# Queries by kv as one float32r pass a head, with the high and low parts stacked in the rows, from the sixth chunk on

## The chip, the core and the metric

The kernel runs on one core of a Trainium2 chip. The core has five engines that work side by side and wait for each other by semaphores: TensorE (PE in the profile; PEld is its loading of weights), VectorE (DVE), ScalarE (ACT), GpSimd (POOL) and SyncE (SP, which issues the DMAs here). TensorE writes to PSUM, eight banks of 2 KB in each of 128 partitions. The metric is the device time of one execution in microseconds (us); less is better.

## What is computed

Linear attention (8 batches, 8 heads, 576 positions, head size 64), then a gated feed-forward block without an activation (model size 512, inner size 1536). Positions of all batches in a row are 4608 tokens.

```python
q_s = softmax(q, over the head's 64 entries)
k_s = softmax(k, over the 576 positions)
kv  = einsum('bhsd,bhse->bhde', k_s, v)          # 64 x 64 a head
x   = einsum('bhsd,bhde->bhse', q_s, kv)         # tokens x 512
out = ((x @ w_a) * (x @ w_b)) @ w_out
```

## The kernel before, in words

**Chunks.** The 4608 tokens are worked through in nine chunks `c` = 0 to 8 of T = 512 tokens; a batch has 576, so all chunks but the first and the last straddle two batches. While TensorE does the feed-forward block of chunk `c`, the attention of chunk `c + 1` is done beside it. "The sixth chunk" is `c = 5`; its attention runs while chunk 4 is multiplied.

**Two float32r parts.** A float32r matmul takes one pass over the columns but keeps fewer bits than float32. So each operand is split (`split`, L338) into a high part (ScalarE copies it into a float32r tile) and a low part (VectorE subtracts the high part from the source), and a product is three passes: high by high, high by low, low by high.

**A chunk's multiplication.** A chunk's loop (L1392) runs over NI = 6 pairs `i` of inner blocks, and in each pair seven products of the Strassen-Winograd kind, 12 matmuls of 256 columns each (`product`, L829), go into three PSUM banks: `kx` (bank k0), `ky` and then `kp` (both bank k1) and `ka` (bank k2). Program order within a pair: attend slice; kx by A11; ky by S2; u2 = ky + kx (L1443 on ScalarE, L1444 on VectorE); ka by S3; u3 (L1447); twelve matmuls of an output projection (`run_pending`, into po0 to po3); attend slice; kp by S1; kx by A12; VectorE's and ScalarE's use of both (L1461 to L1464); another projection; attend slice; kp by S4; L1474 and L1475; ka by A22; L1479 and L1480, and the splits of the gated result. The four remaining banks are po0 to po3; the attention work has one bank, `at`.

**Attention in slices.** `attention_tasks(c)` (L918) returns a list of slices, each a list of steps; `Spread` (L984) hands one slice to each "attend" place of the loop: three a pair, fifteen a chunk, numbered 0 to 14 here (the last pair has none). Slice 3n is at the head of pair n, 3n + 1 in its middle, 3n + 2 in its third place. VectorE's instructions of a slice are queued behind the loop's last VectorE instruction before it (`issue_after`). In slices 0 to 5 keys and values of a new batch are loaded and turned into kv (`key_steps`, `kv_two` L615), and the queries' statistics are taken (`q_stats` L669; `q_stats_out` L682 writes minus the row maxima and the reciprocal sums to DRAM, as `dq`). From the fifth chunk on (`c > 3`) the rest lies so: in slices 8 to 11, for the four head pairs g = 0 to 3, `q_rows` (four DMAs `mr<-dq` that spread maxima and reciprocal sums over the partitions) and `q_turned` (queries with the head's entries in the partitions); in slices 10 to 13 `q_exp` (add the maxima, L722; exponential, L723; split); in slices 11 to 14 `x_product` (L752: three passes with kv's high and low parts as weights; two heads lie side by side in the 128 rows, and kv is a block-diagonal 128x128 matrix made with `mask`) into bank `at`, and L960, where VectorE multiplies by the reciprocal sums into `xf`.

**Order.** For chunks 0 to 2 the order of every engine's queue is written out by hand (`ORDER`, `arrange`). For later chunks the framework's planner sets it at build time, by program order and by its own estimate of when an instruction is ready; on the chip each queue runs in that order. Tiles of one tag share slots (`Slots`), and a new tile waits for the readers of the slot's last one.

Of the kernel before, what the change touches and what calls it, by code (L numbers as in the profile page):

```python
# [255 lines left out]
def linear_attention_then_gated_ffn(  # L256
# [40 lines left out]
    TT = T // P  # L297
    NCH = NT // T
    LATE = NCH - qt_late.shape[0]

    const = ctx.enter_context(tc.tile_pool(name="const", bufs=1))
    sb = ctx.enter_context(tc.tile_pool(name="sb", bufs=2))
# [35 lines left out]
    def split(hi, lo, src, hi_engine="act"):  # L338

        if hi_engine == "act":  # L340
            nc.scalar.copy(out=hi, in_=src)  # L341
        else:
            nc.vector.tensor_copy(out=hi, in_=src)
        return nc.vector.tensor_tensor(out=lo, in0=src, in1=hi.bitcast(F32), op=ALU.subtract)  # L344
# [270 lines left out]
    def kv_two(b, g, kts, vts, tag):  # L615

        pk = ps.tile([P, 2, D + 1], F32, name="pk", tag=tag)
        for n in range(2):
            kv_sums(kts[n], vts[n], tag, pk[:, n])
        den = sb.tile([P, 2], F32, name="den2")  # L620
        nc.vector.tensor_scalar_add(den, pk[:, :, D], EPS)
        nc.vector.reciprocal(out=den, in_=den)
        kv = sb.tile([P, 2, P], F32, name="kv2", bufs=1)
        for n in range(2):
            nc.vector.scalar_tensor_tensor(
                out=kv[:, n].rearrange("p (h d) -> p h d", h=2),
                in0=pk[:, n, 0:D].unsqueeze(1).broadcast_to([P, 2, D]), scalar=den[:, n:n + 1],
                in1=mask.rearrange("p (h d) -> p h d", h=2), op0=ALU.mult, op1=ALU.mult,
            )
        split(*kv_home(b, g), kv, "dve")  # L630


    wholes = sb.tile([P, 2, NP, P], F32, name="wholes", tag="mr", bufs=2)
# [61 lines left out]
    def roomy(c):  # L695
        return c > LATE

# [23 lines left out]
    def q_exp(c, qt, rows):  # L721
        nc.vector.tensor_tensor(out=qt, in0=qt, in1=rows[0], op=ALU.add)  # L722
        nc.scalar.activation(out=qt, in_=qt, func=AF.Exp)  # L723
        if roomy(c):
            hl = sb.tile([P, 2, T], F32R, name="qhl", tag="mr", bufs=2)
            qh, ql = hl[:, 0], hl[:, 1]
        else:
            qh = sb.tile([P, T], F32R, name="qh", bufs=1)
            ql = sb.tile([P, T], F32R, name="ql", bufs=1)
        split(qh, ql, qt)  # L730
        return qh, ql
# [10 lines left out]
    def x_whole(c, g, qw, tag):  # L742

        t0 = c * T
        b0, b1 = t0 // S, (t0 + T - 1) // S
        n0 = min(T, (b0 + 1) * S - t0)
        px = ps.tile([P, T], F32, name="px", tag=tag)
        for b, s in ((b0, slice(0, n0)), (b1, slice(n0, T)))[:b1 - b0 + 1]:
            nc.tensor.matmul(px[:, s], whole[b, g], qw[:, s], start=True, stop=True)  # L749
        return px  # L750

    def x_product(c, g, qhl, tag="at"):  # L752
        qh, ql = qhl
# [164 lines left out]
    def attention_tasks(c):  # L918
# [3 lines left out]
        if c == 2:  # L922
            steps = [(tasks[8][4],)] + steps
            steps[0] += tuple(lambda g=g: kv_split_whole(1, g) for g in range(NP))
            for g in (1, 2, 3):
                load, soft, turn, back, prod = late_key_task(g, "at")
                steps.append((
                    load, lambda soft=soft, turn=turn: (soft(), turn()),
                    lambda back=back, prod=prod: (back(), prod()),
                ))  # L930
        stats, last, turned, rows = [], [], [], []
        every = {}
        for g in range(NP):
# [22 lines left out]
                box["e"] = q_exp(c, box["q"], box["r"])  # L956

            def b2(g=g, box=box):
                px = x_product(c, g, box["e"])
                nc.vector.tensor_tensor(out=xfs[c][:, g], in0=px, in1=box["r"][1], op=ALU.mult)  # L960

# [4 lines left out]
        seq = []  # L966
        for i in range(max(len(stats), len(steps))):
            seq.append((stats[i] if i < len(stats) else []) + (steps[i] if i < len(steps) else []))
        last = pipeline(last)
        if c > 3:  # L970
            begin = 3 * NI - 3 - len(last) - 2
            seq += [[] for _ in range(len(seq), begin)]
            for g in range(NP):
                seq[begin + g:begin + g + 1] = [rows[g:g + 1] + turned[g:g + 1]]
            for n, now in enumerate(last):
                seq[begin + n + 2:begin + n + 3] = [(seq[begin + n + 2] if n + 2 < NP else []) + now]
            return seq
# [414 lines left out]
    for c in range(1, NCH):  # L1392
# [5 lines left out]
        for n, i in enumerate(pairs):  # L1398
            def part(name):
                return named(f"{name}.{(c - 1) * NI + n}") if c < 5 else nullcontext()  # L1400
# [51 lines left out]
            if not end:  # L1452
                with part("proj"):
                    run_pending()
            with part("attend"):
                attend(c > 2 and last)
            kp = ps.tile([P, 2, H], F32, name="kp", tag="k1")
            multiply(kp, S1, T1, True)
            multiply(kx, A12, B21, False)
            with part("pair"):  # L1460
                nc.vector.tensor_tensor(out=cc[:, 3], in0=kp, in1=u3, op=ALU.add)  # L1461
                nc.scalar.copy(out=cc[:, 0, 0], in_=kx[:, 0])  # L1462
# [4 lines left out]
                    run_pending()  # L1467
            if po is None:
                po = [ps.tile([P, DM], F32, name=f"po{t}") for t in range(TT)]
            with part("attend"):  # L1470
                attend(c > 2 and last)
            multiply(kp, S4, B22, False)
# [65 lines left out]
```

## Time and profile before

| | |
|---|---|
| time, median of 3 runs | 936.92 us (936.4 to 938.07) |
| profiled execution, its own time | 935.81 us |
| its span, first to last instruction | 934.0 us |
| TensorE busy | 924.7 us, 6565 matmuls |
| VectorE busy | 618.0 us, 1218 instructions |
| ScalarE busy | 394.0 us, 1094 instructions |
| GpSimd busy | 107.9 us, 88 instructions |
| HBM read and written | 213.09 MB and 36.93 MB |

The page of the profile gives busy time by engine, the chain of work that ended last, and the costliest groups of instructions with the idle time before them and what ended it. Other views of the same trace are used below: the groups by line and shape, the waits, the timeline of one engine (rows: start, time, engine, line, operation, out<-in, shape, count, and in brackets the idle time before and what ended it), and the busy time of each engine in chosen windows.

### The profile page before, as it was taken

What the parts mean: (1) busy time and instruction counts of PE and PEld (TensorE: products, weight loads), DVE (VectorE), ACT (ScalarE), POOL (GpSimd) and SP (SyncE); (2) the same over time, 40 slices, a digit from 0 to 9 for tenths busy, and PEclk for the clock granted to TensorE, in tenths of its full rate; (3) what the DMA queues carried; (4) which work ended last, traced back from release to release, by engine and by line L of the source; (5) the groups of instructions that cost most, each with busy time, mean ns of one, the idle gap of its engine ahead of it and who ended that gap; (6) DMA issues with size and microseconds to landing.
All of it is one profiled execution on the core that took longest, in us unless ns stands there. A gap on an engine that the chain in (4) does not pass through costs nothing.

```text
span 934.0 us, 17535 instructions
## 1 busy us (share of the span) xinstructions
PE 924.7 (99%) x6565; PEld 835.2 (89%) x6565; DVE 618.0 (66%) x1218; ACT 394.0 (42%) x1094; POOL 107.9 (12%) x88
## 2 busy tenths in 40 slices
PE   8999999999999999999999999999999999999998
PEld 6677789999988999999999999999999999999997
DVE  7998898788854677467656574666657454753433
ACT  8988774435521345133613271324424352322111
POOL 1654434330000000000100010000000000000000
PEclk9999999999999999999999999999999999999999
DMA  9989889989788879983989289945997389627761
GB/s 349 349 308 367 333 321 337 330 310 285 266 305 291 259 270 345 283 330 110 337 255 380 94 302 297 361 169 198 331 320 247 102 293 308 219 96 270 248 224 47
DMA packets 88947, 253.27 MB, mean 271 GB/s; under 512 B 10720, under 2 KB 11296, under 8 KB 88864
## 3 DMA queue, kind: packets, MB, share of 16 engines
q1 hardware_dynamic: 88864, 252.16, 78.5%
q8 instruction: 52, 0.85, 0.4%
q14 instruction: 31, 0.25, 0.1%
HBM read 213.09 MB, written 36.93 MB: 268 GB/s over the span
## 4 chain that ended last, share of the span: by engine, by line
PE 95%; DVE 2%; DMA 1%; ACT 0%; POOL 0%; issue 0%; SPq 0%; DVEq 0%; POOLq 0%
PE po L864 31%; PE kx L835 14%; PE kp L835 14%; PE ka L835 14%; PE pt L805 7%; PE ky L835 7%; PE px L761 2%; PE pk L582 2%; PE po L850 1%; PE px L749 1%; DMA kt_first<-in_kt 1%; DVE xo L344 0%; POOL mx L512 0%; DVE kt L544 0%; DVE mc L1128 0%
## 5 line engine op out<-in xcount | busy, mean ns | idle before, releaser
L864 PE MATMUL po<-wo_w,gh 128*128 128x512 f32 x840 | 264.5, 396 | 0.0
L835 PE MATMUL kx<-xo,ws 128*128 128x256 f32 x1152 | 184.7, 282 | 0.3 <-DVE cc L1463 0.2
L835 PE MATMUL ka<-xo,ws 128*128 128x256 f32 x1152 | 177.7, 282 | 0.7 <-DVE u L1447 0.4
L835 PE MATMUL kp<-xo,ws 128*128 128x256 f32 x1152 | 174.8, 283 | 0.5 <-DVE cc L1461 0.5
L864 PEld LDWEIGHTS po<-wo_w,gh 128*128 128x128 f32 x840 | 151.3, 188 | 25.1 <-ACT gh L341 0.5
L835 PEld LDWEIGHTS kx<-xo,ws 128*128 128x128 f32 x1152 | 160.7, 189 | 6.7 <-DVE cc L1463 0.7
L835 PEld LDWEIGHTS ka<-xo,ws 128*128 128x128 f32 x1152 | 157.9, 189 | 6.7 <-issue 0.6
L835 PEld LDWEIGHTS kp<-xo,ws 128*128 128x128 f32 x1152 | 155.7, 189 | 5.8 <-DVE cc L1461 0.8
L864 PE MATMUL po<-wo_w,gl 128*128 128x512 f32 x420 | 153.0, 396 | 0.0
L341 ACT CAST gh<-cc 128x512 fp32r<-128x512 f32 x96 | 58.6, 620 | 168.8 <-DVE cc L1475 145.4
L1462 ACT COPY cc<-kx 128x256 f32<-128x256 f32 x48 | 17.8, 372 | 177.6 <-PE kx L835 170.4
L864 PEld LDWEIGHTS po<-wo_w,gl 128*128 128x128 f32 x420 | 78.0, 188 | 15.7 <-DVE gl L344 0.4
L1474 DVE TENSOR_TENSOR cc<-kp,u 128x512 f32<-128x512 f32 x48 | 33.1, 690 | 86.0 <-PE kp L835 85.9
L805 PE MATMUL pt<-xo,ws 128*128 128x512 f32 x288 | 87.0, 418 | 0.0
L835 PE MATMUL ky<-xo,ws 128*128 128x256 f32 x576 | 86.6, 281 | 0.0
L675 ACT ACTIVATE qt<-qt,st 128x64 f32<-128x64 f32 x224 | 75.3, 340 | 19.6 <-DVE st L672 18.7
L835 PEld LDWEIGHTS ky<-xo,ws 128*128 128x128 f32 x576 | 76.8, 189 | 1.1
L344 DVE TENSOR_TENSOR gl<-cc,gh 128x512 fp32r<-128x512 f32 x96 | 67.1, 704 | 12.9 <-ACT gh L341 12.8
L1461 DVE TENSOR_TENSOR cc<-kp,u 128x512 f32<-128x512 f32 x48 | 33.2, 691 | 62.7 <-PE kp L835 62.2
L805 PEld LDWEIGHTS pt<-xo,ws 128*128 128x128 f32 x288 | 52.9, 188 | 17.3 <-issue 4.2
L512 POOL PARTITION_ALL_REDUCE mx<-m x20 | 18.1, 910 | 433.0 <-DVE m L523 433.0
L1443 ACT COPY u<-kx 128x512 f32<-128x512 f32 x48 | 28.0, 583 | 51.5 <-PE kx L835 48.0
(150 smaller groups left out, 1117.3 us busy)
## 6 DMA issues: line engine op xcount, KB each, us to landing
ws<-dw SPq DMA_DIRECT2D x260, 512.0 KB, 6.0
dw<-ws SPq DMA_DIRECT2D x42, 512.0 KB, 6.6
mr<-dq SPq DMA_DIRECT2D x112, 128.0 KB, 6.0
raw<-in_w_ab SPq DMA_DIRECT2D x24, 512.0 KB, 7.8
out<-ot SPq DMA_DIRECT2D x36, 256.0 KB, 4.7
vt<-in_v SPq DMA_DIRECT2D x28, 325.0 KB, 6.1
qt<-in_q SPq DMA_DIRECT2D x32, 256.0 KB, 5.1
kt<-in_k SPq DMA_DIRECT2D x24, 320.0 KB, 5.3
```

The source lines that it names most:

```text
L341: nc.scalar.copy(out=hi, in_=src)
L344: return nc.vector.tensor_tensor(out=lo, in0=src, in1=hi.bitcast(F32), op=ALU.subtract)
L512: nc.gpsimd.partition_all_reduce(out_ap=mx, in_ap=kv_max(kt), channels=P, reduce_op=bass_isa.ReduceOp.max,)
L582: nc.tensor.matmul(pk[h * D:(h + 1) * D], kt[:, j, h], vt[:, j, h], start=(j == 0), stop=(j == J - 1),)
L675: nc.scalar.activation(out=qt[:, j, h], in_=qt[:, j, h], func=AF.Exp, bias=st[:, h, 0, j:j + 1], accum_out=st[:, h, 1, j:j + 1],)
L761: nc.tensor.matmul(px[:, s], w, m[:, s], start=(i == 0), stop=(i == 2))
L805: nc.tensor.matmul(pt, w[:, wp], x[g][:, xp], start=(g == 0 and i == 0), stop=(g == NP - 1 and i == 2),)
L835: ins = nc.tensor.matmul(pt[:, n], w[:, n, wp, c], x[:, xp, c], start=(first and n == 0 and i == 0), stop=(i == 5), skip_group_check=True,)
L864: ins = nc.tensor.matmul(po[t], a[:, ts], wo[f][:, w], start=(f == ends[0] and i == 0), stop=(f == ends[1] and i == 2),)
L1443: nc.scalar.copy(out=u2, in_=kx)
L1461: nc.vector.tensor_tensor(out=cc[:, 3], in0=kp, in1=u3, op=ALU.add)
L1474: nc.vector.tensor_tensor(out=cc[:, 1], in0=kp, in1=u2, op=ALU.add)
```

## The change

- From `c = 5` on, `q_exp` writes one tile a head h: the high part of the head's 64 rows into these rows, the low part into the other 64 rows (four half-height instructions instead of two of full height).
- `kv_tall` makes matching weights for each head: in the head's own rows the high part of kv beside its low part, in the other rows the high part again beside zeros. `kv_two` leaves out the mask; `kv_again` rebuilds the weights of the batch that the sixth chunk shares with the fifth.
- `x_tall` replaces `x_product`: for each head one pass a batch, instead of three passes for both heads together. The result's own 64 rows and the other 64 rows have to be added: ScalarE copies the other rows out of PSUM (into the tile of the maxima, used up by then) and VectorE adds. Then L960's multiplication takes both heads at once from SBUF.
- The second bank that this needs is bank k1 in a pair's middle slice and k0 in its third slice. To this end kx by A12 stands ahead of kp by S1 in chunks 4 to 8.
- For `c >= 5` products are in slices 8, 10, 11, 13 (before: 11 to 14), `q_exp` one slice earlier each (7, 9, 10, 12; before 10 to 13), rows and turned queries in slices 6, 7, 8, 10 (before 8 to 11).

```diff
+    TALL = 5
@@ in kv_two, after the reciprocal
+        if b * S >= TALL * T:
+            kv = sb.tile([P, 2, P], F32, name="kv2", bufs=1)[:, :, 0:D]
+            nc.vector.tensor_tensor(
+                out=kv, in0=pk[:, :, 0:D], in1=den.unsqueeze(2).broadcast_to([P, 2, D]), op=ALU.mult,
+            )
+            kv_tall(b, g, [(kv[own(h)], None) for h in range(2)])
+            return
@@ new functions
+    def own(h):
+        return slice(h * D, (h + 1) * D)
+    def kv_tall(b, g, heads):
+        q = g // 2
+        w = [sb.tile([P, 2, P], F32R, name=f"kvt{x}{q}", tag=f"kv{x}{q}") for x in "hl"]
+        for n in (2 * q, 2 * q + 1):
+            kvs[b, n] = tuple(t[:, n % 2] for t in w)
+        for h, (hi, lo) in enumerate(heads):
+            me, it = own(h), own(1 - h)
+            nc.vector.tensor_copy(out=w[h][me, :, me], in_=hi)
+            nc.scalar.copy(out=w[h][it, :, me], in_=hi)
+            if lo is None:
+                nc.vector.tensor_tensor(
+                    out=w[h][me, :, it], in0=hi, in1=w[h][me, :, me].bitcast(F32), op=ALU.subtract
+                )
+            else:
+                nc.vector.tensor_copy(out=w[h][me, :, it], in_=lo)
+            nc.gpsimd.memset(w[h][it, :, it].bitcast(F32), 0.0)
+    def kv_again(b):
+        for g in range(0, NP, 2):
+            kvh, kvl = kv_parts[b, g // 2]
+            kv_tall(b, g, [[x.bitcast(F32)[own(h), :, own(h)] for x in (kvh, kvl)] for h in range(2)])
@@ in q_exp, after the exponential
+        if c >= TALL:
+            hl = sb.tile([P, 2, T], F32R, name="qhl", tag="mr", bufs=2)
+            for h in range(2):
+                split(hl[own(h), h], hl[own(1 - h), h], qt[own(h)])
+            return hl
@@ new, in x_product's place for c >= TALL
+    def x_tall(c, g, hl, rows, xf):
+        t0 = c * T
+        edge = min((t0 // S + 1) * S - t0, T)
+        for h, tag in enumerate((at["spare"], "at")):
+            px = ps.tile([P, T], F32, name=f"px{h}", tag=tag)
+            for s in (slice(0, edge), slice(edge, T))[:1 + (edge < T)]:
+                nc.tensor.matmul(
+                    px[:, s], kvs[(t0 + s.start) // S, g][h], hl[:, h, s], start=True, stop=True
+                )
+            me = own(h)
+            nc.scalar.copy(out=rows[0][me], in_=px[own(1 - h)])
+            nc.vector.tensor_tensor(out=xf[me], in0=px[me], in1=rows[0][me], op=ALU.add)
+        nc.vector.tensor_tensor(out=xf, in0=xf, in1=rows[1], op=ALU.mult)
@@ in attention_tasks
+        if c == TALL and c * T % S:
+            steps = [(lambda: kv_again(c * T // S),)] + steps
+            if c >= TALL:
+                seq += [[] for _ in range(len(seq), 3 * NI - 3)]
+                for g, n in enumerate((8, 10, 11, 13)):
+                    exp, mul = every["last"][g]
+                    n_load = max(n - 3, 6)
+                    seq[n_load] = seq[n_load] + [rows[g], turned[g]]
+                    seq[n - 1] = seq[n - 1] + [exp]
+                    seq[n] = [mul] + seq[n]
+                return seq
@@ in the loop over pairs
+            at["spare"] = "k1"
             with part("attend"):
                 attend(c > 2 and last)
+            if c + 1 >= TALL:
+                multiply(kx, A12, B21, False)
             kp = ps.tile([P, 2, H], F32, name="kp", tag="k1")
             multiply(kp, S1, T1, True)
-            multiply(kx, A12, B21, False)
+            if c + 1 < TALL:
+                multiply(kx, A12, B21, False)
...
+            at["spare"] = "k0"
             with part("attend"):
                 attend(c > 2 and last)
             multiply(kp, S4, B22, False)
```

More of the change, by code (lines that the diff above doesn't have):

```diff
@@ L958, in b2 @@
             def b2(g=g, box=box):
+                if c >= TALL:
+                    x_tall(c, g, box["e"], box["r"], xfs[c][:, g])
+                    return
                 px = x_product(c, g, box["e"])
@@ L968, in attention_tasks @@
             seq.append((stats[i] if i < len(stats) else []) + (steps[i] if i < len(steps) else []))
+        every["last"] = last
         last = pipeline(last)
         if c > 3:
+            if c >= TALL:
+                seq += [[] for _ in range(len(seq), 3 * NI - 3)]
[6 more added lines that the diff above has]
+                return seq
             begin = 3 * NI - 3 - len(last) - 2
```

## The prediction

> **What bounds the kernel now.** First the page: its span, the busy shares, and the chain of work that ended last.
>
> ```profile
> span 934.0 us, 17535 instructions
> PE 924.7 (99%) x6565; PEld 835.2 (89%) x6565; DVE 618.0 (66%) x1218; ACT 394.0 (42%) x1094; POOL 107.9 (12%) x88
> PE 95%; DVE 2%; DMA 1%; ACT 0%; POOL 0%; issue 0%; SPq 0%; DVEq 0%; POOLq 0%
> ```
>
> TensorE is busy 99% of the span and makes 95% of the last chain. Then the busy time by engine in the four stretches in which the attention of chunks 5 to 8 is done beside the multiplication of chunks 4 to 7 (window, its length, then busy us of PE, PEld, DVE, ACT, POOL, with counts).
>
> ```profile
> 436.00:535.00 99.00, 99.00 (x753) 91.87 (x752) 62.71 (x130) 36.31 (x111) 3.72 (x4) 1.00 0.78 267
> 535.00:635.00 100.00, 100.00 (x755) 93.22 (x754) 63.53 (x130) 36.66 (x111) 3.73 (x4) 1.00 0.77 264
> 635.00:735.00 100.00, 100.00 (x757) 92.93 (x757) 63.70 (x131) 36.70 (x111) 3.72 (x4) 1.00 0.76 256
> 735.00:831.00 96.00, 96.00 (x663) 89.07 (x663) 54.53 (x104) 34.00 (x107) 0.00 (x0) 1.00 0.70 231
> ```
>
> TensorE never rests there; VectorE has some 36 us free of 99, ScalarE 63. The granted clock is 1.00. Last, TensorE's waits over the whole span; outside of the start this is the longest (one time, 0.5 us).
>
> ```profile
> PE kp L835 <- DVE cc L1461: 0.5, 1, 0.5
> ```
>
> So a matmul taken out of this part shortens the run by its pitch (start to start), as long as nothing new makes TensorE wait. That decides this change: it takes matmuls away and adds work to the two engines that have room, in places where TensorE depends on them.
>
> The Trainium skill (Perfetto Trace Analysis, section Identifying the Most-Contended Engine) warns that a busy share of matmuls is no measure of the headroom of TensorE, since they are pipelined. By that rule the 99% alone proves nothing; the near absence of waits, above, and the even pitches, below, speak for TensorE all the same.
>
> **What is removed.** The timeline of TensorE around one query product in each stretch: its first row, and the first row of what follows.
>
> ```profile
> 497.99 0.45 PE L761 MATMUL px<-qhl,kvh 128*128 128x320 f32 x2
> ...
> 498.73 1.57 PE L835 MATMUL kp<-xo,ws 128*128 128x256 f32 x12
> ...
> 597.46 0.52 PE L761 MATMUL px<-qhl,kvh 128*128 128x384 f32 x2
> ...
> 598.27 0.69 PE L835 MATMUL kp<-xo,ws 128*128 128x256 f32 x4
> ...
> 697.04 0.56 PE L761 MATMUL px<-qhl,kvh 128*128 128x448 f32 x2
> ...
> 697.89 0.84 PE L835 MATMUL kp<-xo,ws 128*128 128x256 f32 x5
> ...
> 794.15 0.62 PE L761 MATMUL px<-qhl,kvh 128*128 128x512 f32 x2
> ...
> 794.84 0.28 PE L835 MATMUL ka<-xo,ws 128*128 128x256 f32 x1
> ```
>
> One head pair's product holds TensorE for 0.74, 0.81, 0.85 and 0.69 us: three passes over 512 columns, in one or two pieces. Afterwards it is two passes over the same pieces, with weights of the same 128x128 form, so a third goes: 0.25, 0.27, 0.28 and 0.23 us. Four head pairs a chunk: 4 x 1.03 = **4.1 us** off TensorE. Nothing else on TensorE changes in number.
>
> The Trainium skill (TensorE: Matmul & The Clock Gate, section Wait — 56ns, not 53.3ns?) gives a warm matmul's start to start as its columns at 2.4 GHz plus about 2.5 ns. By that, sixteen passes of 512 columns are an estimated 3.5 us; the rows give 0.23 us a pass (794.15 to 794.84 for three), a little more, and the measurement is taken.
>
> **What is added, beside TensorE.** Groups by line and shape (busy, mean ns): VectorE's low part (both sources in SBUF) and ScalarE's high part, the multiplication by the reciprocal sums (one source in PSUM), a ScalarE copy out of PSUM, and two VectorE copies out of PSUM of 64 and of 128 rows.
>
> ```profile
> L344 DVE TENSOR_TENSOR qhl<-qtt,qhl 128x512 fp32r<-128x512 f32 x24 | 16.6, 690 | 15.8 <-ACT qhl L341 15.7
> L341 ACT CAST qhl<-qtt 128x512 fp32r<-128x512 f32 x24 | 14.9, 620 | 0.6
> L960 DVE TENSOR_TENSOR xf<-px,mr 128x512 f32<-128x512 f32 x28 | 19.3, 689 | 24.5 <-PE px L761 19.2 <-DMA ws<-dw 3.8 <-DMA kt<-in_k 0.9
> L1443 ACT COPY u<-kx 128x512 f32<-128x512 f32 x48 | 28.0, 583 | 51.5 <-PE kx L835 48.0 <-DVE cc L1474 1.8 <-DVE kvl L344 1.7
> L688 DVE COPY sst<-pst 64x128 f32<-64x128 f32 x7 | 2.0, 281 | 12.1 <-PE pst L686 12.1
> L569 DVE COPY kt<-pkb 128x128 f32<-128x128 f32 x4 | 1.1, 285 | 0.4 <-PE pkb L567 0.4
> ```
>
> The trace has no half-height instruction of 512 elements. The last two rows bound it: 64 rows take 281 ns where 128 take 285, so I charge half height at the full price; at the other end, half of it. Per head pair VectorE gets one more subtraction and two additions (3 x 0.69 = 2.1 us), ScalarE one more cast and two copies (0.62 + 2 x 0.58 = 1.8 us). That is 8.3 and 7.1 us a chunk, well inside the free time above. The weights of `kv_tall` replace a split of the same size by instructions of 64 rows (some 0.3 us each, by the 281 ns row), in slices where TensorE is not waiting for them: nothing. `kv_again` happens once, some eight short VectorE instructions, 2 to 3 us, chunk 4's first slice: between 0 and 1 us on the path, taken as 0.
>
> Averages don't decide, places do. Busy time in pairs 2, 3 and 4 of chunk 5:
>
> ```profile
> 569.40:585.20 15.80, 15.80 (x134) 14.69 (x131) 6.84 (x16) 1.98 (x4) 0.00 (x0) 1.00 0.97 280
> 585.20:602.30 17.10, 17.10 (x121) 16.05 (x120) 10.54 (x19) 5.12 (x9) 0.00 (x0) 1.00 1.04 353
> 602.30:619.60 17.30, 17.30 (x122) 16.22 (x122) 12.28 (x22) 6.08 (x11) 0.00 (x0) 1.00 0.76 286
> ```
>
> Counting VectorE's instructions of `q_exp` and of the product by slice: pair 2 goes from 0 to 6, pair 3 from 5 to 12, pair 4 from 7 to 6. At 0.69 us: 6.84 + 4.1 = 11.0 of 15.8 us, 10.54 + 4.8 = 15.3 of 17.1, 12.28 - 0.7 = 11.6 of 17.3. **Pair 3 becomes tight for VectorE (90%)**, with a slack pair on each side.
>
> **New waits.** (a) In slices 10 and 13 the first product lies in bank k1, and kp by S1 waits until ScalarE has copied and VectorE has added: 0.58 + 0.69 = 1.3 us after the product. Behind these instructions nothing else of TensorE's stands but the second product (about 0.25 us) and the moved kx by A12; twelve such matmuls take 1.44 us by these rows:
>
> ```profile
> 477.07 1.60 PE L835 MATMUL kp<-xo,ws 128*128 128x256 f32 x12
> 478.51 1.20 PE L835 MATMUL kx<-xo,ws 128*128 128x256 f32 x9
> ```
>
> Cover 1.7 against 1.3: a margin of 0.4 us, if both engines are free when the product ends. If one instruction is in the way it is gone by 0.2 to 0.3. Eight such places. (b) In slices 8 and 11 the first product lies in k0; the readers of kx are done long before, and the next kx comes after kp by S4 and ka by A22, 2 x 1.44 = 2.9 us: covered. (c) With kx ahead of kp, L1461 comes up to 1.1 us later; kp by S4 waits for it, behind a projection of twelve matmuls (2.8 us, twelve at 0.23): covered. Of kx's twelve matmuls only nine (the row of 478.51) come behind kp there: the planner already puts three of them first.
>
> (d) **Row maxima.** The DMAs of the first head pair, and VectorE in pair 2 of chunk 4:
>
> ```profile
> 467.50 0.47 SPq L690 DMA_DIRECT2D dq<-sst  x1
> ...
> 470.19 8.24 SPq L716 DMA_DIRECT2D mr<-dq  x8
> DMA to landing us min/median/max: 3.8/7.3/8.8
> 474.15 0.69 DVE L1447 TENSOR_TENSOR u<-ka,u 128x512 f32<-128x512 f32 x1
> 478.71 0.69 DVE L1461 TENSOR_TENSOR cc<-kp,u 128x512 f32<-128x512 f32 x1 [3.87 <-PE kp L835]
> ```
>
> SyncE already issues them at 470.2, right after `dq`; naming slice 6 can't make that much earlier, so no SP queue is newly blocked. They land around 472.0 + 7.3 = 479.3 (fourth issue some 1.8 us after the first). Slice 7, behind L1447, could use them at 474.8. If the planner queues the addition there, VectorE stands until 479.3 instead of 478.7: L1461 is late by 0.6 + 0.7 = 1.3 us, its projection still covers it, and slice 8's product comes after about 482.6 (0.7 + 0.63 + 2 x 0.62 + 0.7 later). Bounds 0 and 1 us a chunk; taken as 0.25.
>
> **Sum.** Minus 4.1; plus (a) half a margin lost at a time, 8 x 0.1 = 0.8; plus (d) some 0.2 to 0.3. About **-3.1 us**. The profiled execution took 935.81 us, 1.8 above its span, so it would come to 932.7; the median of the runs shown is 1.1 higher than that execution, so I predict 936.92 - 3.1 = **933.8 us**.
>
> **Rivals.**
>
> 1. *The gain is eaten by readers of the px banks.* VectorE, at 90% in pair 3 and strictly in order, or ScalarE, comes to the readers one instruction late (0.69 us): each of eight places costs 0.3, and pair 3's general lag about as much in three of four chunks: 936.9 - 4.1 + 2.4 + 1 = 936.2. For it: pair 3's load; against: the planner has hidden such hand-overs almost without a wait so far.
> 2. *Slower: the hand-over of bank k1 in slices 10 and 13.* If both engines are each an instruction behind (0.69 + 0.62 = 1.3), kp by S1 waits 0.9 us, eight times: 7.3 us, and the run takes 936.9 - 4.1 + 7.3 = 940.1. It decides from 0.5 us of wait a place (4.1 / 8), that is from readers 0.9 us late.
> 3. *No gain at all.* If the pitch of the matmuls that follow is held by something that removed passes don't shorten (weight loads are busy 89%), it stays at 936.9. The even pitches speak against it. The Trainium skill's warning above, of busy shares, would allow it.
> 4. *Full gain:* nothing waits and the spread-out slices remove the last small waits: 936.9 - 4.1 - 0.5 = 932.3.
>
> **How the numbers follow.** Forecast, around 933 to 935: 50%. Rival 1: 22%. Rival 2 and smaller forms of it above 938.8: 15%. Rival 3: 5%. Rival 4: 8%. A run of this kernel can tell 0.2% (1.9 us) from no change. Faster by more than that (below 935.05): the forecast, rival 4 and 0.01 of rival 1, 0.59; slower: rival 2 and 0.02 of rival 1, 0.17; within it the rest, 0.24. Range 932.0 to 939.2: it takes in the full gain, rival 1 and rival 3, and leaves out some 0.03 below and most of rival 2, 0.13, above.
>
> **What would show it.** Right: 56 matmuls of px where chunks 5 to 8 had 84, about 8.2 us of them by pitch instead of 12.4; 48 more VectorE instructions there; no wait of kp for ScalarE or VectorE over 0.5 us; L722 not waiting for `mr<-dq` by more than 2 us. Wrong: waits of TensorE in pairs 3 and 4 that add up to more than 2 us, kp by S1 waiting for the px addition, kx by A11 of pair 3 waiting for slice 8's, or half-height instructions that take more than the full-height ones.

## The result: slower, by about 1%

The changed kernel took 945.8 us (median of six runs, 943.25 to 949.52) against 936.85 us for the kernel before beside it (six runs, 935.62 to 938.07): a ratio of 1.0097, with a 95% interval of 1.0075 to 1.012. Forecast was 933.8, with a range up to 939.2. The profiled execution took 943.25 us, the fastest of the six; 7.4 us above the profiled execution of before.

**The page of the profile after** (span; busy time; the last chain by engine):

```profile
span 941.3 us, 17611 instructions
PE 927.1 (98%) x6537; PEld 834.2 (89%) x6537; DVE 652.4 (69%) x1280; ACT 430.8 (46%) x1158; POOL 111.3 (12%) x104
PE 89%; DVE 6%; DMA 3%; issue 1%; ACT 1%; POOL 0%; SPq 0%; DVEq 0%; POOLq 0%
```

TensorE ran 28 matmuls fewer and is still at 98%. That line alone hides the loss. The chain shows it: TensorE's share fell from 95% to 89%, VectorE's rose from 2% to 6%.

**The removed matmuls are gone.** The windows of before, for the px matmuls alone (busy us and count of PE, PEld, DVE, ACT):

```profile
436.00:535.00 99.00, 3.15 (x16) 2.47 (x16) 5.50 (x8) 4.66 (x8) 1.00 0.77 267
...
735.00:831.00 96.00, 3.22 (x8) 1.51 (x8) 5.50 (x8) 4.66 (x8) 1.00 0.69 231
```

Four windows hold 16 + 16 + 16 + 8 = 56, where before had 84.

**Where the time went.** TensorE's waits in chunks 4 to 7 of the changed kernel, 437 to 840 us; the same view of before has no row at all:

```profile
PE px L799 <- DVE qhl L345: 1.6, 3, 0.5
PE kp L890 <- DVE cc L1535: 1.5, 3, 0.7
PE ky L890 <- DVE cc L1549: 1.1, 5, 0.5
PE kx L890 <- ACT qhl L342: 0.6, 1, 0.6
PE px L799 <- DVE u L1514: 0.4, 1, 0.4
```

(Line numbers after: L890 is the product, L799 a tall pass, L803 ScalarE's copy, L804 VectorE's addition, L805 the multiplication, L1535 the sum that takes in kp by S1, before L1461, and L1549 the one that takes in kp by S4, before L1474.) A wait lengthens the distance from start to start by more than its own time: the 0.42 us ahead of kp at 606.36 us (below) made it 0.58 us longer than usual. So I also counted stalls by starts: of each two neighbouring matmuls, the time from start to start less the median for that form, where more than 0.06 us is left, added up over pairs 3 and 4 of chunks 4 to 7. That gives 9.8 us after and 0.5 before. Of the 9.8 us, 2.3 lie ahead of matmuls of kp, 2.8 ahead of ky, 3.0 ahead of px and 1.5 ahead of kx. And it closes: 4.1 us fewer matmuls, 9.3 us more stalls, 5.2 us longer by reckoning; measured by ScalarE's copies of kx, from pair 5 of chunk 3 to pair 0 of chunk 8, it took 5.6 us longer. The other 1.7 us of the profiled difference arose ahead of the fourth chunk, where both kernels do the same (last section).

**The place is pair 3.** Busy time in pairs 2, 3 and 4 of chunk 5 after, same columns as in the prediction:

```profile
569.40:589.00 19.60, 19.60 (x171) 18.34 (x170) 12.23 (x26) 5.74 (x11) 0.00 (x0) 1.00 0.80 253
589.00:609.30 20.30, 19.88 (x141) 18.57 (x141) 16.95 (x29) 11.83 (x20) 0.40 (x2) 1.00 1.00 395
609.30:626.00 16.70, 16.00 (x109) 14.54 (x108) 13.70 (x24) 5.12 (x9) 0.40 (x2) 1.00 0.60 206
```

Pair 3 was to hold 15.3 us of VectorE's work in 17.1; it holds 16.95 in 20.3. Now TensorE through it (the output projection's rows left out), first before, then after:

```profile
592.17 1.59 PE L835 MATMUL kp<-xo,ws 128*128 128x256 f32 x12
593.61 1.24 PE L835 MATMUL kx<-xo,ws 128*128 128x256 f32 x9
...
598.27 1.64 PE L835 MATMUL kp<-xo,ws 128*128 128x256 f32 x12
599.75 1.59 PE L835 MATMUL ka<-xo,ws 128*128 128x256 f32 x12
601.17 0.40 PE L835 MATMUL kx<-xo,ws 128*128 128x256 f32 x2
...
602.21 1.40 PE L835 MATMUL kx<-xo,ws 128*128 128x256 f32 x10
603.45 1.59 PE L835 MATMUL ky<-xo,ws 128*128 128x256 f32 x12
```

```profile
599.65 0.41 PE L799 MATMUL px<-qhl,kvth 128*128 128x384 f32 x2
...
600.92 1.11 PE L890 MATMUL ka<-xo,ws 128*128 128x256 f32 x8
601.88 0.39 PE L799 MATMUL px<-qhl,kvth 128*128 128x384 f32 x2
602.11 0.69 PE L890 MATMUL ka<-xo,ws 128*128 128x256 f32 x4
602.64 1.59 PE L890 MATMUL kp<-xo,ws 128*128 128x256 f32 x12
604.07 0.40 PE L799 MATMUL px<-qhl,kvtl 128*128 128x384 f32 x2
604.30 1.64 PE L890 MATMUL ka<-xo,ws 128*128 128x256 f32 x12
606.36 1.69 PE L890 MATMUL kp<-xo,ws 128*128 128x256 f32 x12 [0.42 <-DVE cc L1535]
607.94 1.66 PE L890 MATMUL kx<-xo,ws 128*128 128x256 f32 x12
610.14 0.47 PE L799 MATMUL px<-qhl,kvtl 128*128 128x384 f32 x2 [0.55 <-DVE qhl L345]
610.77 1.70 PE L890 MATMUL ky<-xo,ws 128*128 128x256 f32 x12 [0.16 <-DVE cc L1549]
```

Bank k1 holds, in turn, kp by S1, kp by S4 and the next ky, and VectorE has to read each before the next may be written. Before, kp by S1 stands 7 us into the pair (592.17, from 585.2) and a whole projection lies between it and kp by S4; behind that, ka by A22, a product and the next kx give 3.7 us until ky. After, k1 is lent to px at 599.65, and the planner queued kp by S1 behind both projections and ka by A22, 13.6 us into the pair (602.64, from 589.0). Nothing waits there. But what used to lie between the three users of k1 is spent: it takes the next pair's ka by S3 (604.30) as filler, and kp by S1, its sum, kp by S4, its sum and ky become a nearly bare chain: one product of twelve matmuls is left in each gap (ka, then kx). VectorE in that stretch:

```profile
600.71 1.41 DVE L804 TENSOR_TENSOR xf<-px,mr 64x512 f32<-64x512 f32 x2 [2.12 <-ACT mr L803]
602.15 0.69 DVE L805 TENSOR_TENSOR xf<-xf,mr 128x512 f32<-128x512 f32 x1
...
603.49 0.68 DVE L833 TENSOR_TENSOR xt<-xf 128x512 f32<-128x512 f32 x1
...
605.62 0.69 DVE L1535 TENSOR_TENSOR cc<-kp,u 128x512 f32<-128x512 f32 x1
606.22 0.69 DVE L345 TENSOR_TENSOR xo<-xt,xo 128x512 fp32r<-128x512 f32 x1
...
607.15 1.41 DVE L804 TENSOR_TENSOR xf<-px,mr 64x512 f32<-64x512 f32 x2
608.59 1.40 DVE L345 TENSOR_TENSOR qhl<-qtt,qhl 64x512 fp32r<-64x512 f32 x2
610.03 0.69 DVE L1549 TENSOR_TENSOR cc<-kp,u 128x512 f32<-128x512 f32 x1
```

VectorE stood 2.12 us for ScalarE's copy at 598.6 to 600.7 (which itself had waited for px up to 600.1), and then never rests up to 610.7. kp by S1 ended at 604.2, its sum starts at 605.6; kp by S4 ended at 608.05, its sum starts at 610.03, behind two additions and two subtractions of the new work. Those delays are what TensorE waits for. The experiments ask which of the three makes the loss: the load, the standing for ScalarE, or the chain on k1.

### The profile page after: what moved, and what is told of

Same layout as the page of the kernel before. It is cut to its first block, busy times and chain, and to the rows that moved or that the text cites. A ratio compares the mean times of both kernels' runs of the same rounds, so it can differ in the third digit from the quotient of the medians.

```text
span 941.3 us, 17611 instructions
## 1 busy us (share of the span) xinstructions
PE 927.1 (98%) x6537; PEld 834.2 (89%) x6537; DVE 652.4 (69%) x1280; ACT 430.8 (46%) x1158; POOL 111.3 (12%) x104
## 4 chain that ended last, share of the span: by engine, by line
PE 89%; DVE 6%; DMA 3%; issue 1%; ACT 1%; POOL 0%; SPq 0%; DVEq 0%; POOLq 0%
PE po L919 30%; PE kx L890 13%; PE kp L890 13%; PE ka L890 13%; PE pt L860 7%; PE ky L890 7%; PE pk L583 2%; DMA ws<-dw 1%; PE po L905 1%; PE px L816 1%; PE px L789 1%; DMA qtt<-in_q_late 1%; DVE xo L345 1%; DVE qhl L345 1%; DVE xf L804 1%
## 5 line engine op out<-in xcount | busy, mean ns | idle before, releaser
L890 PE MATMUL kx<-xo,ws 128*128 128x256 f32 x1152 | 181.0, 282 | 1.0 <-ACT qhl L342 0.6
L890 PE MATMUL ka<-xo,ws 128*128 128x256 f32 x1152 | 179.5, 283 | 0.7 <-DVE u L1517 0.4
L890 PE MATMUL kp<-xo,ws 128*128 128x256 f32 x1152 | 172.1, 282 | 2.0 <-DVE cc L1535 2.0
L890 PEld LDWEIGHTS kx<-xo,ws 128*128 128x128 f32 x1152 | 159.1, 189 | 7.4 <-ACT qhl L342 0.8
L890 PEld LDWEIGHTS ka<-xo,ws 128*128 128x128 f32 x1152 | 158.6, 189 | 7.0 <-issue 0.6
L890 PEld LDWEIGHTS kp<-xo,ws 128*128 128x128 f32 x1152 | 154.1, 189 | 7.0 <-DVE cc L1535 2.9
L919 PE MATMUL po<-wo_w,gl 128*128 128x512 f32 x420 | 150.8, 396 | 0.0
L919 PEld LDWEIGHTS po<-wo_w,gl 128*128 128x128 f32 x420 | 77.9, 188 | 15.3 <-DVE gl L345 0.4
L890 PE MATMUL ky<-xo,ws 128*128 128x256 f32 x576 | 87.8, 283 | 1.1 <-DVE cc L1549 1.1
L890 PEld LDWEIGHTS ky<-xo,ws 128*128 128x128 f32 x576 | 76.8, 189 | 3.6 <-DVE cc L1549 2.3
L1549 DVE TENSOR_TENSOR cc<-kp,u 128x512 f32<-128x512 f32 x48 | 33.1, 689 | 65.1 <-PE kp L890 64.8
L1535 DVE TENSOR_TENSOR cc<-kp,u 128x512 f32<-128x512 f32 x48 | 33.1, 690 | 32.3 <-PE kp L890 31.9
```

What stands on the lines that cost most here:

```text
L890: ins = nc.tensor.matmul(pt[:, n], w[:, n, wp, c], x[:, xp, c], start=(first and n == 0 and i == 0), stop=(i == 5), skip_group_check=True,)
L919: ins = nc.tensor.matmul(po[t], a[:, ts], wo[f][:, w], start=(f == ends[0] and i == 0), stop=(f == ends[1] and i == 2),)
L1549: nc.vector.tensor_tensor(out=cc[:, 1], in0=kp, in1=u2, op=ALU.add)
```

## The experiments

Each ran beside the kernel before on the same chip. Ratios are to it, with 95% intervals; edits are against the changed kernel unless said otherwise. "Stalls" are those in pairs 3 and 4 of chunks 4 to 7 counted as above (before: 0.5 us).

### The pieces that are free: slices, swap, load

New slices with the old product (TALLX = 99 turns off tall weights, tall product and swap):

```diff
-        if c >= TALL:
+        if c >= TALLX:
             hl = sb.tile([P, 2, T], F32R, name="qhl", tag="mr", bufs=2)
```

> The slices alone: products of chunks 5 to 8 in slices 8, 10, 11, 13, exponentials one slice earlier, row maxima from slice 6, with the old three-pass product in one bank, the old drain and the old order of kx and kp. Theory A (VectorE and ScalarE have too much to do in pair 3, because of the added half-height instructions): the places cost little, 935 to 939 us. Theory B (the new places and the earlier row maxima are themselves what costs): most of the 9 us, 942 to 946 us.

Measured 937.38 us, 1.0003 (0.9993 to 1.0012): nothing.

The swap alone, in the kernel before:

```diff
+            if c + 1 >= 5:
+                multiply(kx, A12, B21, False)
             kp = ps.tile([P, 2, H], F32, name="kp", tag="k1")
             multiply(kp, S1, T1, True)
-            multiply(kx, A12, B21, False)
+            if c + 1 < 5:
+                multiply(kx, A12, B21, False)
```

> Only kx by A12 ahead of kp by S1 in chunks 4 to 8, all else as before the change. Theory A: nothing, 936 to 938 us. Theory C (the swap delays kp's sum on VectorE and with it the next products): 940 us or more.

Measured 937.2 us, 1.0004 (0.9995 to 1.0013): nothing.

The load on VectorE alone: new slices, old product, and spare half-height additions behind it, eight a chunk; then one more in each exponential, twelve a chunk, as many as the change adds.

```diff
+                if c >= TALL:
+                    for h in range(2):
+                        r = [box["r"][w][own(h)] for w in range(2)]
+                        nc.vector.tensor_tensor(out=r[0], in0=r[0], in1=r[1], op=ALU.add)
```

> The new slices with the old three-pass product (which alone took 937.4 us), and behind each product two more half-height VectorE additions, on rows that are used up: 8 VectorE instructions a chunk, with no ScalarE work, no bank and nobody waiting for them. If VectorE's number of instructions in these places is the cause: 941 to 944 us. If it is the chain over ScalarE and the banks: 937 to 938.5 us.

> The new slices with the old product, two spare half-height VectorE additions behind each product (as the earlier run with 8 a chunk, 936.7 us) and one more in each exponential step: 12 spare VectorE instructions a chunk, as many as the change adds, with no ScalarE work and no chain. If VectorE's number of instructions alone fills pair 3 (it was at 14.5 busy us of 17.2 there with 24 instructions, 28 would be 17): 939 to 942 us. If the queue's waits for ScalarE are needed as well: 936.5 to 938 us.

Measured 936.73 us, 1.0015 (1.0005 to 1.0024), and 937.17 us, 1.0004 (0.9995 to 1.0013): little or nothing with eight, nothing with twelve. Pair 3 of chunk 5 with twelve spares:

```profile
587.20:604.70 17.50, 17.50 (x123) 16.45 (x123) 15.37 (x27) 5.60 (x10) 0.00 (x0) 1.00 1.02 401
```

VectorE is at 88% there, near the 90% forecast for the change, and TensorE doesn't lose a moment. The number of instructions alone is not the cause.

### The drain in parts

Without any drain (the multiplication reads the second pass alone), with only the borrowed bank read, without ScalarE's copies, and with ScalarE's copies but without VectorE's additions:

```diff
-            me = own(h)
-            nc.scalar.copy(out=rows[0][me], in_=px[own(1 - h)])
-            nc.vector.tensor_tensor(out=xf[me], in0=px[me], in1=rows[0][me], op=ALU.add)
-        nc.vector.tensor_tensor(out=xf, in0=xf, in1=rows[1], op=ALU.mult)
+        nc.vector.tensor_tensor(out=xf, in0=px, in1=rows[1], op=ALU.mult)
```

> The change, but the result of the second head's pass alone is multiplied by the reciprocal sums: the two ScalarE copies and the two half-height additions a head pair are left out, and the first pass has no reader. Theory A: with 8 VectorE and 8 ScalarE instructions a chunk fewer, and no chain behind the banks, most waits of TensorE go: 932 to 937 us. Theories B and C: 942 to 946 us.

```diff
+            if h == 0:
+                nc.vector.tensor_tensor(out=xf, in0=px, in1=rows[1], op=ALU.mult)
```

> As the kernel without the drain, but the one multiplication reads the first head's pass, in the borrowed bank k0 or k1, and the second pass has no reader. If the hold of the borrowed bank costs by itself (the wait at kp by S1 in slices 10 and 13 that the prediction's second rival had): 3 to 7 us more than there, 940 to 944 us. If not: 936 to 938 us.

```diff
-            nc.scalar.copy(out=rows[0][me], in_=px[own(1 - h)])
```

> The change without ScalarE's copies of the other rows: the additions read the unchanged row maxima instead (so half of each sum is left out), VectorE's instruction count is that of the change, and it waits for TensorE alone. If it is the chain TensorE, ScalarE, VectorE at the head of VectorE's queue that costs: 937 to 940 us. If it is the number of VectorE instructions: 943 to 946 us.

```diff
             nc.scalar.copy(out=rows[0][me], in_=px[own(1 - h)])
-            nc.vector.tensor_tensor(out=xf[me], in0=px[me], in1=rows[0][me], op=ALU.add)
-        nc.vector.tensor_tensor(out=xf, in0=xf, in1=rows[1], op=ALU.mult)
+        nc.vector.tensor_tensor(out=xf, in0=px, in1=rows[1], op=ALU.mult)
```

> The change without VectorE's two additions a head pair: ScalarE copies as in the change, and VectorE multiplies the second pass alone (so the first head's result and the sums are left out). If VectorE's instructions cost: 936 to 939 us, near the kernel without any drain. If ScalarE's copies and the hold of the banks by them cost: 942 us or more.

| what is left of the drain | us | ratio (95%) | stalls |
|---|---|---|---|
| one multiplication, second pass | 936.61 | 1.0003 (0.9993 to 1.0012) | 2.7 |
| one multiplication, borrowed bank | 936.92 | 0.9992 (0.998 to 1.0004) | 3.5 |
| VectorE's part | 941.12 | 1.0039 (1.0024 to 1.0054) | 7.8 |
| ScalarE's part, one multiplication | 941.69 | 1.0046 (1.0029 to 1.0063) | 7.4 |
| all of it (the change) | 945.8 | 1.0097 (1.0075 to 1.012) | 9.8 |

So the whole loss hangs on the drain, and each engine's part brings about half of it. Borrowing the bank is not dear in itself if one instruction frees it. With that shortest hold TensorE still has kp by S1 behind the projections, but VectorE comes to its sum sooner, and a product is left to cover the next step, as the timeline of pair 3 of chunk 5 shows:

```profile
600.41 1.59 PE L888 MATMUL kp<-xo,ws 128*128 128x256 f32 x12
...
602.78 1.69 PE L888 MATMUL kp<-xo,ws 128*128 128x256 f32 x12 [0.55 <-DVE cc L1533]
604.31 1.58 PE L888 MATMUL ka<-xo,ws 128*128 128x256 f32 x12
605.73 1.59 PE L888 MATMUL kx<-xo,ws 128*128 128x256 f32 x12
607.16 1.59 PE L888 MATMUL ky<-xo,ws 128*128 128x256 f32 x12
```

Here the next pair's ka by S3 still stands between kp by S4 and ky, where the change had used it one place earlier.

### Moving work off VectorE, or elsewhere in time

Each of these gives VectorE less to do, or fewer instructions ahead of its sums. All were slower than the kernel before.

```diff
-        nc.vector.tensor_tensor(out=xf, in0=xf, in1=rows[1], op=ALU.mult)
+        nc.gpsimd.tensor_tensor(out=xf, in0=xf, in1=rows[1], op=ALU.mult)
```

> The change, with the last multiplication by the reciprocal sums on GpSimd instead of VectorE: 4 VectorE instructions a chunk fewer, and the drain of the banks as it was. Theory A in the form 'VectorE's total load': a third of the added load goes, 941 to 944 us. If it is the drain of the banks or the queue ahead of it that counts: 945 us, unchanged.

Measured 948.57 us, 1.0115 (1.009 to 1.014); stalls 15.5 us, some 3 of them from matmuls at half clock (last section).

```diff
-        nc.vector.tensor_tensor(out=qt, in0=qt, in1=rows[0], op=ALU.add)
+        (nc.gpsimd if c >= TALL else nc.vector).tensor_tensor(out=qt, in0=qt, in1=rows[0], op=ALU.add)
```

> The change with the addition of the row maxima on GpSimd: four full-height VectorE instructions a chunk fewer, ahead of the exponential, where no bank is held. If VectorE's load in pair 3 is the cause, about a third goes as with the other instructions left out: 941 to 944 us. If a longer chain to the split counts more (GpSimd took 1.3 us for such an instruction, VectorE 0.7): 946 us or more.

Measured 946.04 us, 1.0098 (1.0062 to 1.0134). Stalls in pairs 3 and 4 fell to 4.4 us, but kx now waited 5.3 us for the additions of slice 8's px (bank k0). GpSimd takes 1.29 us for what took VectorE 0.69:

```profile
481.34 1.29 POOL L757 TENSOR_TENSOR qtt<-qtt,mr 128x512 f32<-128x512 f32 x1 [0.37 <-DMA mr<-dq]
```

Both on GpSimd (the reciprocal sums taken in ahead of the split, since the product is linear), exponentials two slices ahead, products in 10, 11, 13, 14:

```diff
+            nc.gpsimd.tensor_tensor(out=qt, in0=qt, in1=rows[1], op=ALU.mult)
...
-                for g, n in enumerate((8, 10, 11, 13)):
+                for g, n in enumerate((10, 11, 13, 14)):
```

> The change with both full-height steps on GpSimd: the row maxima added there, and the multiplication by the reciprocal sums done there too, before the split instead of after the sum; exponentials two slices ahead of the products, which are in slices 10, 11, 13, 14. VectorE has 16 instructions a chunk instead of 24 (12 before the change). If VectorE's load in pair 3 is the cause: 933 to 938 us, level with the kernel before or under it. If not: 943 us or more.

Measured 954.23 us, 1.0197 (1.0175 to 1.0219). TensorE's waits in chunks 4 to 7 now include 4.5 us of kx for ScalarE's copy into u and 4.6 us of ky for the sum of kp by S4.

ScalarE empties both halves of each bank (four copies a head pair), and VectorE adds and multiplies at full height, from SBUF, one slice later:

```diff
-            nc.vector.tensor_tensor(out=xf[me], in0=px[me], in1=rows[0][me], op=ALU.add)
+            nc.scalar.copy(out=xf[me], in_=px[me])
+    def x_join(rows, xf):
+        nc.vector.tensor_tensor(out=xf, in0=xf, in1=rows[0], op=ALU.add)
```

> The change with VectorE taken out of the drain: ScalarE copies both halves of each pass out of PSUM (four half-height copies a head pair instead of two), and VectorE adds and multiplies at full height from SBUF one slice later, when the copies are long done (two instructions a head pair instead of three). VectorE then never stands at the head of its queue for a product. If those waits, together with the work behind them, are the loss: 934 to 938 us. If ScalarE's part of the chain, or the split ahead of the products, is: 941 us or more.

Measured 956.58 us, 1.0202 (1.0156 to 1.0248), the worst; stalls 19.7 us (some 3 of them again at half clock), mostly of px waiting for `qhl` and of ky waiting for the sum of kp by S4.

The preparation of the next chunk's operands (L833 and the splits of `xo`, which the earlier products draw into pair 3) kept behind the loop's VectorE work; products of the last two head pairs later; and both:

```diff
-                    x_operands(xfs[c + 1], early, xo)
+                    with tc.issue_after(last.ins) if c + 1 >= 5 else nullcontext():
+                        x_operands(xfs[c + 1], early, xo)
```

> The change, with VectorE's preparation of the next chunk's operands (x_operands) queued behind VectorE's work of pair 4 (early ones) and behind u3 of pair 5 (late ones) for chunks 5 to 8, so that none of it can stand in pairs 3 and 4. Theory D (the products that now come earlier draw this preparation forward into pair 3, where the added drains and splits already fill VectorE's queue, and sums that TensorE needs come late): about half of the loss goes or more, 938 to 942 us. Theory A without this (the added instructions alone are too many): 944 to 947 us, unchanged.

```diff
-                for g, n in enumerate((8, 10, 11, 13)):
+                for g, n in enumerate((8, 10, 13, 14)):
```

> The change with the products in slices 8, 10, 13, 14 instead of 8, 10, 11, 13: pair 3 has one product and one exponential fewer, pair 4 one of each more. If pair 3's crowding is the cause, the waits there shrink: 938 to 942 us. If the load counts wherever it lies: 944 to 948 us, with the waits of TensorE moved to pair 4 and 5.

> Both shifts together: products in slices 8, 10, 13, 14, and the next chunk's operands kept out of pairs 3 and 4. VectorE would then have some 20 instructions in pair 3 and 24 or fewer in the others. If a pair is slowed only where VectorE's busy time and its waits at the head of the queue fill it: 935 to 938 us. If each such chain costs wherever it stands: 940 us or more.

Measured 946.86 us, 1.0117 (1.0083 to 1.0151); 940.66, 1.005 (1.0035 to 1.0065); 941.71, 1.0058 (1.0038 to 1.0078). Pinning changed the kind of wait, not the sum, as the waits of the first of these show:

```profile
PE kx L890 <- DMA ws<-dw: 4.3, 3, 1.8
PE ky L890 <- DVE cc L1551: 2.9, 8, 0.6
```

Later products spread the load and won back half, yet slices 10 and 13 still borrow k1, and ky still waited 2.8 us for the sum of kp by S4.

### Which bank is lent

Three versions make the tall product for head pairs 0 and 1 only (2.05 us fewer matmuls); head pairs 2 and 3 keep the old product, in slices 12 and 13. First in slices 8 and 10 (k0, then k1); second the same with the drain by `x_join`; last in slices 8 and 11, so that only k0 is ever lent.

```diff
-        if c >= TALL:
+        if c >= TALL and g < 2:
...
-                for g, n in enumerate((8, 10, 11, 13)):
+                for g, n in enumerate((8, 10, 12, 13)):
```

> The change for the head pairs 0 and 1 only (slices 8 and 10); head pairs 2 and 3 keep the three-pass product, in slices 12 and 13. Half of TensorE's gain (2 us), half of the added instructions, 8 of VectorE's own in pair 3 instead of 12. If pair 3's filling is the cause: 934.5 to 936.5 us, level with the kernel before or a little under it. If each chain costs by itself, half of the loss: 940 to 942 us.

> The same drain for head pairs 0 and 1 alone (slices 8 and 10), the three-pass product for the others in slices 12 and 13 (with the change's own drain such a kernel took 942.1 us). If VectorE's waits for products are the loss: 934 to 937 us. If not: 940 us or more.

```diff
-                for g, n in enumerate((8, 10, 12, 13)):
+                for g, n in enumerate((8, 11, 12, 13)):
```

> The tall product is made for head pairs 0 and 1 alone, both in third slices (8 and 11), so that only bank k0 is ever borrowed; head pairs 2 and 3 go by the old product in slices 12 and 13. Theory F (the borrowed k1 in the middle slice pushes kp by S1 behind the projections, and kp by S1, its sum, kp by S4, its sum and the next ky become a bare chain on one bank): 935 to 938 us, and kp by S1 stands ahead of the second product pass again. Rival (the drain costs wherever it stands, since VectorE's queue stands for ScalarE's copies): 940 to 942.5 us, as with the slices 8 and 10.

| slices of the two tall products | us | ratio (95%) | stalls |
|---|---|---|---|
| 8 (k0) and 10 (k1) | 942.13 | 1.0063 (1.0041 to 1.0084) | 6.2 |
| the same, ScalarE's drain | 940.78 | 1.0034 (1.0019 to 1.0048) | 6.0 |
| 8 (k0) and 11 (k0) | 936.63 | 1.0003 (0.9993 to 1.0013) | 2.0 |

One slice's difference takes the whole loss away. TensorE in pair 3 of chunk 5 in the last version (projections left out), and its only wait in chunks 4 to 7:

```profile
595.83 0.76 PE L890 MATMUL kx<-xo,ws 128*128 128x256 f32 x5
596.42 1.59 PE L890 MATMUL kp<-xo,ws 128*128 128x256 f32 x12
...
602.06 1.59 PE L890 MATMUL kp<-xo,ws 128*128 128x256 f32 x12
603.49 0.76 PE L890 MATMUL ka<-xo,ws 128*128 128x256 f32 x5
...
604.89 1.64 PE L890 MATMUL kx<-xo,ws 128*128 128x256 f32 x12
606.36 1.58 PE L890 MATMUL ky<-xo,ws 128*128 128x256 f32 x12
```

```profile
PE kx L890 <- DMA ws<-dw: 1.4, 1, 1.4
```

kp by S1 is back ahead of the projection, as before, with a projection between it and kp by S4, and a product and kx between kp by S4 and ky. VectorE still stands for ScalarE in pair 3 (4.3 us on average over chunks 4 to 7, against 4.5 in slices 8 and 10), so that standing does no harm by itself. Moving the second product by a slice also takes some instructions out of pair 3 (20.5 of VectorE's on average, against 23.25). Two runs speak against that as the cause: the spare additions were harmless at 25.75 without a lent bank, and the version with later products and pinned preparation, which lends k1 in slices 10 and 13, has 20.5 in pair 3 as well and VectorE standing 4.4 us there, yet took 941.71 us. (It makes all four products tall, so it is no exact twin.) Its only waits of TensorE in chunks 4 to 7 are eight of ky for the sum of kp by S4, one behind each pair that lends k1:

```profile
PE ky L890 <- DVE cc L1551: 5.4, 8, 0.8
```

No version beats the kernel before.

## Why the prediction was wrong

**What bounds the kernel: right.** A matmul taken out pays by its pitch, where nothing new makes TensorE wait. Removed matmuls plus added stalls give the measured change of chunks 4 to 7 (taken up to the first copy of u in chunk 8, as above), in the profiled executions:

```
                         removed  stalls added    sum   measured
the change                 -4.10          9.30   5.20       5.58
borrowed bank, one mult    -4.10          3.00  -1.10      -1.10
no drain                   -4.10          2.19  -1.92      -1.74
slices 8 and 10            -2.05          5.73   3.67       3.99
slices 8 and 11            -2.05          1.51  -0.54      -0.45
twelve spare additions      0.00         -0.22  -0.22      -0.43
```

The count takes in pairs 3 and 4 alone. A version that waits elsewhere needs all six pairs (with the row maxima on GpSimd, -0.2 becomes 11.0 us, against 10.3 measured), and then the sums of the versions with tall products come out some 0.5 to 1.4 us too high.

So rival 3 (no gain from removed passes) falls. The Trainium skill (Perfetto Trace Analysis, section Identifying the Most-Contended Engine) was right in its own way: the busy share stood at 98% while the kernel lost 1%; waits and pitches told what the share didn't.

**What is removed: right**, 28 matmuls and about 4 us: from start to start, the px matmuls of chunks 5 to 8 took 12.5 us before and 9.3 after, of which 0.8 are waits behind them.

**What is added: the price right, the place wrong.** Half height costs full price: two additions of 64x512 took 1.41 us (0.70 each) and two ScalarE copies 1.19, as ScalarE's timeline shows:

```profile
600.09 1.19 ACT L803 COPY mr<-px 64x512 f32<-64x512 f32 x2 [1.96 <-PE px L799]
```

But pair 3 held 16.95 us of VectorE, not 15.3: the count took in the moved slices and not what becomes ready because of them. The second head pair's result now exists in slice 10, and the operand preparation (L833, two splits: 2.1 us) came forward into pair 3. And a busy share leaves out standing: VectorE also stood 2.9 us a pair 3 for ScalarE, on average over chunks 4 to 7. Before, it stood nearly as long, 2.7 us, but with more room beside it.

**New wait (a), bank k1: this is the step that failed.** I priced it as a local wait, 1.7 us of cover against 1.3 of hold, 0.8 us in all. TensorE hardly waits there, for the planner queued kp by S1 after both projections, so the question "how long does kp wait for px" got the answer "not at all", and the price was paid behind it: 5.1 of the 9.8 us of stalls lie ahead of kp and ky, the next two users of the bank, and 4.4 ahead of px and kx, the largest part (1.6 us of waits) for query splits that stand in VectorE's queue behind the same additions (608.59, above). With only k0 lent both kinds go, but for one wait for weights. Rival 2 had the right bank and slices and the right sign; its price, 7.3 us of waits, is near the 9.3 us of stalls, but its mechanism (readers late by an instruction, kp by S1 waiting) was not what happened. The first sign that the prediction named against itself, waits of over 2 us in pairs 3 and 4, came true; "kp by S1 waiting for the px addition" did not.

The Trainium skill (Perfetto Trace Analysis, section Optimization Strategy) reads the same gap repeating on the engine that should be busy as a possible sign of too little buffer room for the next tile. The trace agrees: a gap ends with kp by S4 at 606.4, 707.3 and 804.9 us, in pair 3 of three of the four chunks, and lending out the one PSUM bank that two products already share made it.

**New wait (b), bank k0: right.** Slices 8 and 11 alone cost nothing. **(c), the swap: right**, 1.0004. **(d), row maxima: about right.** VectorE's L757 sat 5.8 us in four times for `mr<-dq` (the longest 2.1, just over the 2 us that the prediction named), with no measurable price for the slices alone, 1.0003. **`kv_again`**, taken as 0: at pair 2 of chunk 4 the change stood 0.04 us ahead of before, counted from chunk 3's last pair.

**Rival 1** (readers of px one instruction late, VectorE at 90%) gave 936.2; the load alone costs nothing, so as stated it falls. What it missed is that, as far as these runs go, lateness matters where a bank has three users in a row.

**What stays open.** The versions without the drain and with the borrowed bank alone gained 1.7 and 1.1 us over chunks 4 to 7 in their profiled executions, and the one with slices 8 and 11 would have had 2.0 but for one wait for weights; no median shows any. The intervals reach about 1 us to either side, so they could hide all but the first of these gains. In the profiled execution without the drain, the part ahead of chunk 4, which the change leaves as it was, took 1.5 us longer, with a mean clock of 0.66 between 10 and 15 us; whether that recurs in the other executions is not known. The weight loads, which the crowded stretches share with the row maxima (DMA share 1.03 in pair 3 of the version with slices 8 and 11), are another suspect; that was not tried. The planner's reason for the new order was not taken apart either.

## What to carry to other kernels

A buffer that is lent out is priced over the whole ring of its users, not at the next one: list who writes it in order, and what independent work lies between each two, after the planner has set its order. Where an in-order engine reads that buffer each time, add what stands in its queue ahead of each reading, including work that the change makes ready earlier. If there is a choice, lend the buffer whose next user is farthest away: here one slice, k0 for k1, was worth 5.5 us. That holds while the readers are prompt: with the row maxima on GpSimd, k0 lent in slice 8 made kx wait 5.3 us.

## What the runs showed of the hardware

**The clock fell inside a busy stretch.** With the multiplication on GpSimd, px waited 1.51 us (at 712.46), ky for 0.16 right after, and then TensorE's granted clock was halved for 3.4 us (columns as in the prediction; the third number from the right is the clock):

```profile
705.00:714.20 9.20, 7.36 (x57) 6.71 (x56) 8.85 (x14) 4.93 (x10) 1.77 (x1) 1.00 0.98 373
714.20:717.60 3.40, 3.40 (x18) 3.40 (x17) 2.37 (x4) 0.48 (x1) 0.00 (x0) 0.50 0.74 260
```

That adds an estimated 1.7 us (half of 3.4) to a stall of 1.8 (9.20 less 7.36), and doubles its price. The same happened at 510 and 616 us in the version with ScalarE's full drain. The Trainium skill (TensorE: Matmul & The Clock Gate, section HAM oscillation — how this bites in real kernels) gives the rule as no idle gaps of TensorE above some 3.4 us; here no single gap came near that (the longest ahead of these was 2.0 us). Nor does such a gap always do it: in the same run gaps of 1.51 and 0.16 us between 507.8 and 509.9 us left the clock at 1.00, and with ScalarE's full drain gaps of some 2 us and 0.8 us that ended at 720.2 and at 819.3 us did too. What decides was not looked into.

**It can fall near the start, too.** In the profiled execution of the change it was at half for 3.4 us, where before had it in full:

```profile
15.70:19.10 3.40, 3.40 (x13) 1.84 (x13) 2.64 (x11) 2.56 (x8) 0.00 (x0) 0.51 1.05 415
```

This belongs to no part of the change, and some executions of the kernel before have a mean clock of 0.998 as well.
